# One set of the fifth group's first dense product by seven block products, in a fused linear-attention and GELU kernel

## The chip, the cores and the metric

The kernel runs on one core of one Trainium2 chip. The metric is device time in microseconds (us) of that core, from a few runs; a profile of one execution stands beside it. A core has four compute engines that run side by side: TensorE (PE in the profile, with its weight loads shown as PEld), VectorE (DVE), ScalarE (ACT) and GpSimd (POOL). SyncE (SP) issues the transfers. Matmuls write into PSUM, which has eight banks; all else lives in SBUF.

## The reference

The input of the dense part is the output of a chunked linear attention with a decay per head. Cut to what matters:

```python
# attention: B=4, H=8, S=768, D=64, blocks of 64
for b in range(nb):
    intra = einsum('bhic,bhjc->bhij', qb, kb) * Dmask        # causal, with decay
    out[b] = einsum('bhij,bhjd->bhid', intra, vb) + einsum('bhid,bhde->bhie', qb * lam_pow, kv_state)
    kv_state = lam_block * kv_state + einsum('bhsd,bhse->bhde', kb * rev_pow, vb)
# dense: 3072 tokens, d_model 512, d_ff 2048
x = out.transpose(0, 2, 1, 3).reshape(3072, 512)
h = x @ w_in                  # the first dense product
g = gelu_tanh(h)
y = g @ w_out                 # the second dense product
```

## The kernel before

The program interleaves the attention of 24 steps (each 256 positions of 4 heads) with the dense part of 7 groups of tokens. The dense work stands in a queue of small pieces, `filler`; `fill(n)` emits n of them between the attention's stages. Groups 3 to 6 have 512 tokens. Group 4 is the fifth, with steps 12 to 15.

A plain piece of the first dense product makes one block of 128 features for all 512 tokens: four matmuls of 512 columns and a gelu on ScalarE.

```python
SEVEN = (5, 6)                       # groups whose first dense product goes by seven products
groups = [[0, 1], [2], [3], [4, 5], [6, 7], [8, 9], [10, 11]]

def mm1(fs):
    Hps = ps_M.tile([P, per, N], FP32, tag="M", name="Hps")
    for i, f in enumerate(fs):
        for c in range(NC):                                   # NC = 4
            pin(nc.tensor.matmul(by_block(Hps[:, i, :]), w_in16[:, c, f * P : (f + 1) * P],
                                 x(c), start=(c == 0), stop=(c == NC - 1)))
    ...
    pin(nc.scalar.activation(out=dst, in_=Hps[:], func=AF.Gelu_apprx_tanh))
```

For groups 5 and 6 the first product is taken as a 2x2 block product with seven multiplications in place of eight (Strassen-Winograd). It needs sums of weight blocks (`sum_win`, made once on VectorE in fp16), four sums of activation blocks per group (`sum_x`), and evictions that add the seven products up. A *set* `k` is two feature blocks of each half. Three PSUM banks hold X, W and Y; three temporaries in SBUF hold what has been read out.

```python
X_FACTORS = {1: ((0, 0), (0, 0)), 2: ((0, 1), (1, 0)), 3: (4, (1, 1)), 4: ((1, 1), 4),
             5: (1, 1), 6: (2, 2), 7: (3, 3)}      # weight block, activation block; 1..4 alone are sums

def sum_x(m):                                      # xs, 4 of 128x512 fp16
    ...
    pin(nc.vector.tensor_tensor(x_block(m, cs), x_block(a, cs), x_block(b, cs), op))

def seven(m, k):
    ...                                            # four matmuls of 256 columns into
    dst = st[{2: "W", 5: "Y", 3: "Y"}.get(m, "X")] # X: 1, 6, 7, 4;  W: 2;  Y: 5, 3
    ...
    def copied(name, tag, eng):                    # a temporary out of the load buffers
        t = ld.tile([P, HH, 2, D], FP32, tag=tag, name=f"{name}_{g}_{k}")
        ...                                        # copy of dst into it, by eng
    if m == 1:   copied("m1", "q32", nc.scalar)
    elif m == 2: added(0, 0, "m1")                 # VectorE: m1 = W + m1; its gelu is kept for later
    elif m == 5: copied("q", "q32", nc.scalar); release()      # release: emits the gelus kept
    elif m == 6: copied("u2", "k32", nc.vector)
    elif m == 3: added(0, 1, "u2")
    elif m == 7: added(1, 1, "q")
    elif m == 4: pending.insert(0, lambda: gelu(1, 0, dst[:]))
    if k == HF // 2 - 1 and m in (3, 7, 4):
        release()
```

The load buffers are four each of `q32`, `k32` and `v32`, 128x512 fp32. They belong to the attention: a step's q, k and v are loaded into them, then cast to fp16 by three engines, transposed by a transfer, and used.

```python
ld = ctx.enter_context(tc.tile_pool(name="ld", bufs=4))
def cast_qk(s):
    ...
    pin(q_eng.tensor_tensor(wide(tq), q32[:], decay(dq, s), ALU.mult))           # VectorE
    pin(nc.scalar.activation(out=wide(tk), in_=k32[:], func=AF.Copy))            # ScalarE
def scale_v(s):
    pin(nc.gpsimd.tensor_tensor(wide(tv[:]), ld32[s][2][:], decay(dv, s), ALU.mult))  # GpSimd
def prep_v(s):       # scales v, then loads step s + 3
def prep_qk(s):      # cast_qk(s), then the transpose by a transfer
```

The second dense product goes by seven products in all these groups. It reads sums of gelu blocks, `gs`, that `sum_g` makes on VectorE: four sums over rows 0 to 3 and the same over rows 4 to 7. `behind(k, ...)` hangs such a sum on the k-th piece of the queue. For group 3 the last addition, `o` from `u` and `q`, is GpSimd's.

`burst(ns, ss)` emits the attention matmuls of two steps at once: scores S of steps `ns`, outputs O of steps `ss`, states K, and more of O; then the masking of S (`PT`, VectorE), the activations `xT` out of O (ScalarE), and the updates of the state: `t` on VectorE, `u` on GpSimd. Instructions keep the order in which they are written on each engine (`pin`). The schedule around group 4:

```python
    R(17, 15)                # its end queues group 4
    fill(1); U(17); fill(1)
    sum_win(3, 0, nc.vector);  fill(2)
    prep(19)
    sum_win(3, 1, nc.vector);  fill(2)
    sum_win(4, 0, nc.vector);  fill(2)
    sum_win(4, 1, nc.vector);  fill(2)
    prep_qk(20);  fill(1)
    prep_qk(21);  prep_v(20);  fill(3)
    burst((18, 19), (16, 17))
    prep_v(21);  fill(2)
    U(18);  U(19);  fill(4)
    prep_qk(22);  fill(2)
    burst((20, 21), (18, 19), 11, 4)         # queues group 5
    fill(3);  U(20);  U(21);  fill(20)
    prep_qk(23);  ...
```

Of the kernel before, what the change touches and what calls it, by code (L numbers as in the profile page):

```python
# [9 lines left out]
FP16 = mybir.dt.float16  # L10
AF = mybir.ActivationFunctionType
# [4 lines left out]
def kernel(  # L16
# [12 lines left out]
    P = 128  # L29
# [114 lines left out]
    def sum_win(m, j, eng):  # L144

        if not wi_sum:
            wi_sum.extend(wst.tile([P, 2, 2, DFF // 2], FP16, tag=f"w{2 + i}", name=f"ws{i}")
                          for i in range(2))
        a, op, b = I_SUMS[m]
        cs, fs = slice(0, 2), slice(512 * j, 512 * j + 512)  # L150
        pin(eng.tensor_tensor(w_in_block(m, cs, fs), w_in_block(a, cs, fs),
                              w_in_block(b, cs, fs), op))
# [96 lines left out]
    def wide(t):  # L249
        return t.rearrange("p j h d -> p h j d")  # L250

    def decay(t, s):
        hs = halves[s % 2]
        return t[:, hs, :].unsqueeze(3).to_broadcast([P, HH, 2, D])

    def prep_v(s):
        scale_v(s)
        if s >= 6:
            if s + 3 == FIRST_DMA_T + 1:
                load_step(s + 3, "qk")  # L260
            else:
                load_ahead(s + 3)
# [6 lines left out]
    def prep_qk(s):  # L269
        cast_qk(s)  # L270
        transpose_dma(s)

    def cast_qk(s):
        q32, k32, _ = ld32[s]
        tqk = a16p.tile([P, 2, 2, HH, D], FP16, tag="qk16", name=f"qk16_{s}")
        tq, tk = tqk[:, 0], tqk[:, 1]
        q_eng = nc.gpsimd if s == 3 else nc.vector
        pin(q_eng.tensor_tensor(wide(tq), q32[:], decay(dq, s), ALU.mult))  # L278
        if s == 0:
            inverse(halves[0])  # L280
            odd(halves[1])
            inverse(halves[1])
        pin(nc.scalar.activation(out=wide(tk), in_=k32[:], func=AF.Copy))  # L283
        a16[s] = (tq, tk)
        whole_qk[s] = tqk

    whole_qk = {}

    def transpose_dma(s):
        tqk = whole_qk.pop(s)  # L290
        if s >= FIRST_DMA_T:
            o = qkp.tile([P, 2, 2, 2, P], FP16, tag="qkT", name=f"qkT_{s}")
            pin(nc.sync.dma_start_transpose(out=o[:].rearrange("p a j h t -> p (a j h) t"),
                                            in_=tqk[:].rearrange("p a j h d -> p (a j h d)")))
            qkT[s] = o
            if s == FIRST_DMA_T:
                load_step(s + 1, "v")
# [219 lines left out]
        return gs_kept[1:]  # L517

    SEVEN = (5, 6)
    SLOTS = {5: {1: 0, 2: 1, 5: 1, 6: 1, 3: 1, 7: 1}, 4: {1: 0, 2: 1, 5: 0, 6: 1, 3: 1, 7: 1}}  # L520
    groups = [[0, 1], [2], [3], [4, 5], [6, 7], [8, 9], [10, 11]]
    group_of = {sb: (g, i) for g, sbs in enumerate(groups) for i, sb in enumerate(sbs)}
# [2 lines left out]
    def queue_group(g, lead=0, per_set=0):  # L525
# [69 lines left out]
        def product(m, p, part=None):  # L595

            st = of_group

            def bank(name):
                if name not in st:  # L600
                    st[name] = ps_M.tile([P, 1 if name == "X" else NP, HE], FP32, tag="M",
                                         name="M" + name[0])
                return st[name]

            if m in (2, 5, 3):
                dst = bank("Y" if m in (5, 3) else "W")[:, p]
            else:
                dst = bank(f"X{p}")[:, 0]
            opens = m == 1 or (m in (2, 5) and p == 0)
            closes = m in (2, 3, 4)  # L610
            a, b = FACTORS[m]
            for i in range(HF) if part is None else range(HF // 2 * part, HF // 2 * part + HF // 2):
                lhsT = g_rows(a, i)[:, p * P : p * P + P]
                if b in W_SUMS:
                    rhs = w_sum16[:, w_slot[b], i, :]
                else:
                    F, E = b
                    rhs = w_out16[:, F * HF + i, E * HE : E * HE + HE]
                pin(nc.tensor.matmul(dst, lhsT, rhs, start=(opens and i == 0),  # L619
                                     stop=(closes and i == HF - 1), skip_group_check=True))  # L620
            if part == 0:
                return
            last = p == NP - 1

            def temp(name):
                if name not in st:
                    st[name] = mtp.tile([P, NP, HE], FP32, tag=name, name=name)
                return st[name]

            def out_tile(T):  # L630
                if f"o{T}" not in st:
                    st[f"o{T}"] = otp.tile([P, NP, 2, HE], FP32, tag="o32", name=f"o{T}")
                return st[f"o{T}"]

            def copy(to, of):
                pin(nc.scalar.activation(out=to, in_=of, func=AF.Copy))  # L636

            def store(T, ps=slice(0, NP), es=slice(0, 2)):
                r = row0 + T * HN
                rows = out[r : r + HN, :].rearrange("(p q) (e d) -> q p e d", q=P, e=2)  # L640
                whole = g == 3
                for i in [ps] if whole else [slice(i, i + 1) for i in range(ps.start, ps.stop)]:
                    pin(nc.sync.dma_start(out=rows[:, i, es], in_=out_tile(T)[:, i, es, :]))

            one = slice(p, p + 1)
            if m == 1:
                copy(temp("m1")[:, p], dst)
            elif m == 2 and last:
                pin(nc.vector.tensor_tensor(out_tile(0)[:, :, 0, :], st["W"][:], st["m1"][:], ALU.add))
            elif m == 5 and last:  # L650
                copy(temp("q")[:], st["Y"][:])
            elif m == 6:
                copy(temp("u2")[:, p], dst)
            elif m == 3 and last:
                pin(nc.vector.tensor_tensor(out_tile(0)[:, :, 1, :], st["Y"][:], st["u2"][:], ALU.add))
                store(0)
            elif m == 7 and last_group:
                pin(nc.vector.tensor_tensor(out_tile(1)[:, p, 1, :], dst, st["q"][:, p], ALU.add))
                if last:
                    store(1, one, slice(1, 2))  # L660
            elif m == 7:
                copy(temp("u3")[:, p], dst)
                if last:
                    pin(nc.gpsimd.tensor_tensor(out_tile(1)[:, :, 1, :], st["u3"][:], st["q"][:],  # L664
                                                ALU.add))
# [32 lines left out]
        def seven(m, k):  # L698
# [48 lines left out]
                added(1, 1, "q")  # L747
            elif m == 4:
                pending.insert(0, lambda: gelu(1, 0, dst[:]))
            if k == HF // 2 - 1 and m in (3, 7, 4):  # L750
                release()

        def merge(lead, per_set):
# [83 lines left out]
        if g in SEVEN:  # L837
# [6 lines left out]
            for k, m in enumerate((2, 4, 3)):  # L844
                behind(len(parts) * k, 4, 8, (m,))
            return
        for i in range(HF):
            for fs in ([[i, i + HF]] if per == 2 else [[i], [i + HF]]):
                filler.append(lambda fs=fs: mm1(fs))
        for m, p in order:  # L850
# [4 lines left out]
        if per == 2:  # L855
            behind(5, 0, 4, (1, 2))
            behind(6, 0, 4, (4, 3))
            behind(7, 4, 8, (1,))
            behind(8, 4, 8, (2,))
            behind(9, 4, 8, (4,))  # L860
            behind(10, 4, 8, (3,))
        else:
            behind(9, 0, 4, (1, 2) if g == 3 else (1, 2, 4, 3))
            if g == 3:
                behind(12, 0, 4, (4, 3))
            w = 2 if g + 1 in SEVEN else 1
# [23 lines left out]
    def U(n):  # L890
        update(n, 1)
# [143 lines left out]
    U(17)  # L1035
    fill(1)
    sum_win(3, 0, nc.vector)
    fill(2)
    prep(19)
    sum_win(3, 1, nc.vector)  # L1040
    fill(2)
    sum_win(4, 0, nc.vector)
    fill(2)
    sum_win(4, 1, nc.vector)
    fill(2)
    prep_qk(20)
# [57 lines left out]
```

## Time and profile before

| what | value |
|---|---|
| time, median of 3 runs | 199.69 us (199.68 to 200.06) |
| span of the profiled execution | 198.0 us, TensorE clock 1.000 |
| TensorE, matmuls | 191.6 us busy, 97% of the span |
| VectorE, ScalarE, GpSimd | 153.9, 123.0, 75.5 us busy (78, 62, 38%) |
| plain first product, one matmul of 512 columns (as recorded) | 379 ns |
| seven-product matmul of 256 columns (as recorded) | 273 ns |
| sum of activations `xs`, VectorE | 0.41 us at the least |
| cast of q, VectorE / copy of 128x512 from PSUM, ScalarE | 0.68 / 0.60 us at the least |

Matmul records overlap, so their durations are not their cost; the distance from start to start is, and it is read from the chain or the timeline. The line of digits gives the busy tenths of an engine in 40 equal slices of the span. In the timeline a line is: start and duration in us, engine, source line, operation, result and operand, shapes and count; a bracket at its end gives the idle time of the engine just before, and what ended it. In the waits a line is: who waited for whom, the sum in us, how often, and the longest. The chain, followed back from the last instruction, gives start, duration and what ran.

### The profile page before, as it was taken

What the parts mean: (1) busy time and instruction counts of PE and PEld (TensorE: products, weight loads), DVE (VectorE), ACT (ScalarE), POOL (GpSimd) and SP (SyncE); (2) the same over time, 40 slices, a digit from 0 to 9 for tenths busy, and PEclk for the clock granted to TensorE, in tenths of its full rate; (3) what the DMA queues carried; (4) which work ended last, traced back from release to release, by engine and by line L of the source; (5) the groups of instructions that cost most, each with busy time, mean ns of one, the idle gap of its engine ahead of it and who ended that gap; (6) DMA issues with size and microseconds to landing.
All of it is one profiled execution on the core that took longest, in us unless ns stands there. A gap on an engine that the chain in (4) does not pass through costs nothing.

```text
span 198.0 us, 5937 instructions
## 1 busy us (share of the span) xinstructions
PE 191.6 (97%) x2439; PEld 140.2 (71%) x2439; DVE 153.9 (78%) x296; ACT 123.0 (62%) x251; POOL 75.5 (38%) x85
## 2 busy tenths in 40 slices
PE   8979999999999999999999999999999999999993
PEld 2546544456888888754588854578888888888882
DVE  4887722789999989969999927998778996588620
ACT  3673878457794675677645377844768836779221
POOL 6594213457557642465563526156002030002000
DMA  6999999999999999989994997400211200030205
GB/s 168 291 323 386 386 387 387 293 289 301 336 263 265 218 307 226 194 252 190 295 205 95 272 316 182 104 16 0 53 66 43 104 10 0 0 107 2 106 14 201
DMA packets 61722, 37.86 MB, mean 191 GB/s; under 512 B 17536, under 2 KB 54656, under 8 KB 61696
## 3 DMA queue, kind: packets, MB, share of 16 engines
q1 hardware_dynamic: 61152, 37.23, 72.9%
q8 instruction: 19, 0.31, 0.7%
q10 hardware_dynamic: 544, 0.26, 0.5%
q14 instruction: 7, 0.06, 0.1%
HBM read 27.26 MB, written 6.29 MB: 169 GB/s over the span
## 4 chain that ended last, share of the span: by engine, by line
PE 88%; SPq 4%; DMA 4%; ACT 1%; issue 1%
PE Hps L542 24%; PE MX L619 17%; PE MY L619 9%; PE HX L711 7%; PE O2ps L557 7%; PE MW L619 4%; DMA wi<-in_moe_w_in_dram 4%; SPq L70 4%; PE HY L711 4%; PE S L340 3%; PE Hps L802 3%; PE HW L711 2%; PE OK L398 2%; PE O L449 1%; PE O L424 1%; PE Tps L311 1%
## 5 line engine op out<-in xcount | busy, mean ns | idle before, releaser
L542 PE MATMUL Hps<-xT,w_in 128*128 128x512 f16 (+1 forms) x288 | 50.8, 332 | 0.0
L501 POOL TENSOR_TENSOR u<-t,lumask 128x256 f16<-128x256 f32 x40 | 31.0, 789 | 46.5 <-DVE t L494 28.4
L542 PEld LDWEIGHTS <-w_in 128*128 128x128 f16 x288 | 27.8, 98 | 19.0
L546 ACT ACTIVATE gT<-Hps 128x512 f16<-128x512 f32 x56 | 33.1, 598 | 9.3 <-PE Hps L542 8.8
L350 DVE TENSOR_TENSOR PT<-S,mask 128x512 f16<-128x512 f32 x48 | 30.3, 681 | 6.5 <-PE S L340 6.4
L619 PEld LDWEIGHTS <-gs 128*128 128x128 f16 x320 | 31.2, 98 | 3.6
L266 POOL TENSOR_TENSOR v<-v,dv 128x512 f16<-128x512 f32 x24 | 30.0, 1254 | 7.4 <-DMA v<-in_v_dram 7.2
L619 PEld LDWEIGHTS <-gT 128*128 128x128 f16 x240 | 23.2, 98 | 3.6 <-ACT gT L546 0.5
L619 PE MATMUL MX<-w_sum,gs 128*128 128x256 f16 x160 | 21.4, 273 | 0.0
L664 POOL TENSOR_TENSOR o<-u,q 128x512 f32<-128x512 f32 (+1 forms) x5 | 5.8, 1158 | 37.9 <-ACT u L636 37.9
L278 DVE TENSOR_TENSOR qk<-q,dq 128x512 f16<-128x512 f32 x23 | 19.7, 859 | 0.6 <-DMA q<-in_q_dram 0.5
L283 ACT ACTIVATE qk<-k 128x512 f16<-128x512 f32 x24 | 15.0, 626 | 6.5 <-DMA k<-in_k_dram 6.4
L589 DVE TENSOR_TENSOR gs<-gT 128x1024 f16<-128x1024 f16 (+1 forms) x24 | 17.6, 737 | 1.5 <-ACT gT L546 1.5
L557 PE MATMUL O2ps<-w_out,gT 128*128 128x512 f16 x64 | 14.6, 379 | 0.0
L475 ACT ACTIVATE xT<-OK 128x256 f16<-128x256 f32 x26 | 10.0, 453 | 7.3 <-PE OK L398 7.1
L711 PEld LDWEIGHTS <-ws 128*128 128x128 f16 x128 | 12.5, 98 | 1.8
L636 ACT ACTIVATE u<-MX 128x256 f32<-128x256 f32 x18 | 6.9, 384 | 10.2 <-PE MX L619 10.2
L475 ACT ACTIVATE xT<-O 128x256 f16<-128x256 f32 x22 | 8.0, 459 | 5.9 <-PE O L449 5.0
L557 PEld LDWEIGHTS <-gT 128*128 128x128 f16 x64 | 6.1, 98 | 6.6
L619 PE MATMUL MY<-w_out,gs 128*128 128x256 f16 x80 | 10.7, 273 | 0.0
L340 PEld LDWEIGHTS <-qkT 64*64 64x64 f16 x384 | 6.0, 106 | 6.5 <-issue 2.5
L589 DVE TENSOR_TENSOR gs<-gs,gT 128x1024 f16<-128x1024 f16 (+1 forms) x12 | 10.2, 851 | 0.3
(95 smaller groups left out, 319.4 us busy)
## 6 DMA issues: line engine op xcount, KB each, us to landing
q<-in_q_dram SPq DMA_DIRECT2D x24, 256.0 KB, 5.0
k<-in_k_dram SPq DMA_DIRECT2D x24, 256.0 KB, 5.2
v<-in_v_dram SPq DMA_DIRECT2D x23, 256.0 KB, 5.4
out_dram<-o SPq DMA_DIRECT2D x19, 256.0 KB, 4.3
wo<-in_moe_w_out_dram SPq DMA_DIRECT2D x4, 1024.0 KB, 9.5
wi<-in_moe_w_in_dram SPq DMA_DIRECT2D x4, 512.0 KB, 7.0
wi<-in_moe_w_in_dram SPq DMA_DIRECT2D x2, 1024.0 KB, 12.8
out_dram<-o SPq DMA_DIRECT2D x2, 512.0 KB, 6.6
```

Of the source, the lines that this page charges most:

```text
L266: pin(nc.gpsimd.tensor_tensor(wide(tv[:]), ld32[s][2][:], decay(dv, s), ALU.mult))
L278: pin(q_eng.tensor_tensor(wide(tq), q32[:], decay(dq, s), ALU.mult))
L283: pin(nc.scalar.activation(out=wide(tk), in_=k32[:], func=AF.Copy))
L350: pin(nc.vector.tensor_tensor(t[:, hl].rearrange("p b c d -> p b (c d)"), Sps[:].rearrange("p b c d -> p b (c d)"), mask[:].unsqueeze(1).t ...
L475: pin(nc.scalar.activation(out=d, in_=o, func=AF.Copy))
L501: pin(nc.gpsimd.tensor_tensor(u[:], state[half][:].unsqueeze(2).to_broadcast([P, 2, 2, D]), lumask[:, 2 * half : 2 * half + 2, :].unsqueez ...
L542: pin(nc.tensor.matmul(by_block(Hps[:, i, :]), w_in16[:, c, f * P : (f + 1) * P], x(c), start=(c == 0), stop=(c == NC - 1)))
L546: pin(nc.scalar.activation(out=dst, in_=Hps[:], func=AF.Gelu_apprx_tanh))
L557: pin(nc.tensor.matmul(O2[tau][0][:], gT[:, f % HF, f // HF, tau * P : (tau + 1) * P], w_out16[:, f, :], start=(n == 0), stop=(n == NF - 1)))
L589: pin(nc.vector.tensor_tensor(g_rows(m, i), g_rows(a, i), g_rows(b, i), op))
L619: pin(nc.tensor.matmul(dst, lhsT, rhs, start=(opens and i == 0), stop=(closes and i == HF - 1), skip_group_check=True))
L711: pin(nc.tensor.matmul(dst[:, i, :], w_in_block(a, slice(c, c + 1), slice(f * P, f * P + P))[:, 0], x_block(b, slice(c, c + 1))[:, 0], sta ...
```

## The change

Set 0 of group 4's first dense product (feature blocks 0, 1, 8 and 9) goes by seven block products, to spare TensorE one multiplication in eight of that set; the other twelve blocks stay plain. The seven pieces are interleaved with plain ones (a 0 in the list is a plain piece), and their gelus are released at once. The rest makes room: the key casts of steps 20 and 21 move forward, the activation sums and the query casts are placed by hand, the transposes of steps 20 and 21 part from their casts, the cast of step 22 moves behind the second burst, the gelu sums of group 4 are hung on other pieces (two of them behind the second burst), and the first output tile of group 3 is stored in two transfers.

```diff
+    def cast_q(s):
+        both16(s)                     # the fp16 tile of q and k, made once
+        q_eng = nc.gpsimd if s == 3 else nc.vector
+        pin(q_eng.tensor_tensor(wide(a16[s][0]), ld32[s][0][:], decay(dq, s), ALU.mult))
+    def cast_k(s):
+        both16(s)
+        pin(nc.scalar.activation(out=wide(a16[s][1]), in_=ld32[s][1][:], func=AF.Copy))
...
+    MIXED = 4
...
-                whole = g == 3
+                whole = g == 3 and T == 1
...
-            if k == HF // 2 - 1 and m in (3, 7, 4):
+            if (k == HF // 2 - 1 or g == MIXED) and m in (3, 7, 4):
                 release()
...
-        for i in range(HF):
+        if g == MIXED:
+            sum_xs.append(sum_x)
+            plain = [[f] for i in range(2, HF) for f in (i, i + HF)]
+            for m in (1, 2, 5, 0, 6, 3, 0, 7, 0, 4):
+                filler.append((lambda m=m: seven(m, 0)) if m else (lambda fs=plain.pop(0): mm1(fs)))
+            for fs in plain:
+                filler.append(lambda fs=fs: mm1(fs))
+        for i in range(HF) if g != MIXED else ():
...
-            behind(9, 0, 4, (1, 2) if g == 3 else (1, 2, 4, 3))
+            n1 += 3 * (g == MIXED)
+            behind(n1 - 7, 0, 4, (1, 2))
             if g == 3:
                 behind(12, 0, 4, (4, 3))
+            else:
+                behind(n1 + 5, 0, 4, (4,))
+                behind(n1 + 9, 0, 4, (3,))
...
     sum_win(3, 0, nc.vector)
+    cast_k(20)
     fill(2)
     prep(19)
     sum_win(3, 1, nc.vector)
     fill(2)
     sum_win(4, 0, nc.vector)
     fill(2)
+    cast_k(21)
     sum_win(4, 1, nc.vector)
-    fill(2)
-    prep_qk(20)
-    fill(1)
-    prep_qk(21)
+    for m in (1, 2, 3, 4):
+        sum_xs[0](m)
+    cast_q(20)
+    transpose_dma(20)
     prep_v(20)
     fill(3)
+    cast_q(21)
+    fill(7)
     burst((18, 19), (16, 17))
+    transpose_dma(21)
     prep_v(21)
-    fill(2)
+    fill(3)
     U(18)
     U(19)
-    fill(4)
-    prep_qk(22)
-    fill(2)
+    fill(3)
     burst((20, 21), (18, 19), 11, 4)
     fill(3)
     U(20)
     U(21)
+    prep_qk(22)
     fill(20)
```

More of the change, by code (lines that the diff above doesn't have):

```diff
@@ L273, in cast_qk @@
     def cast_qk(s):
[L274 to L278, printed above, removed]
+        cast_q(s)
         if s == 0:
@@ L282, in cast_qk, with both16 @@
             inverse(halves[1])
-        pin(nc.scalar.activation(out=wide(tk), in_=k32[:], func=AF.Copy))
-        a16[s] = (tq, tk)
-        whole_qk[s] = tqk
+        cast_k(s)
+    def both16(s):
+        if s in a16:
+            return
+        tqk = a16p.tile([P, 2, 2, HH, D], FP16, tag="qk16", name=f"qk16_{s}")
+        a16[s] = (tqk[:, 0], tqk[:, 1])
+        whole_qk[s] = tqk
+    def cast_q(s):
[5 more added lines that the diff above has]
+        pin(nc.scalar.activation(out=wide(a16[s][1]), in_=ld32[s][1][:], func=AF.Copy))
     whole_qk = {}
@@ L519 @@
     SEVEN = (5, 6)
+    MIXED = 4
+    sum_xs = []
     SLOTS = {5: {1: 0, 2: 1, 5: 1, 6: 1, 3: 1, 7: 1}, 4: {1: 0, 2: 1, 5: 0, 6: 1, 3: 1, 7: 1}}
```

## The prediction, made before the changed kernel had run

> **What bounds the kernel now.** I read the page's head first, then TensorE's waits, then the chain, then VectorE and GpSimd instruction by instruction around the change (110 to 137 us).
>
> ```profile
> PE 191.6 (97%) x2439; PEld 140.2 (71%) x2439; DVE 153.9 (78%) x296; ACT 123.0 (62%) x251; POOL 75.5 (38%) x85
> ...
> PE   8979999999999999999999999999999999999993
> ...
> DVE  4887722789999989969999927998778996588620
> ```
>
> TensorE is busy for 97% of the span and in every slice after the third. A busy matmul record can hide a wait, so the waits of TensorE come next:
>
> ```profile
> PE S L340 <- DVE qkT L316: 0.8, 2, 0.5
> PE idle L181 <- PEq L1088: 0.8, 1, 0.8
> PE OK L398 <- POOL u L501: 0.6, 1, 0.6
> PE Tps L311 <- POOL qk L278: 0.4, 1, 0.4
> PE Hps L802 <- ACT w_in L108: 0.4, 1, 0.4
> ```
>
> That is 3.0 us in all, none of it in the changed stretch. The chain there is TensorE alone, without a gap:
>
> ```profile
> 109.45 3.49 PE MX L619 x32
> 112.95 4.32 PE Hps L542 x20
> 117.26 0.57 PE S L340 x32
> ```
>
> So a matmul removed here is time gained, and any wait put in is time lost: nothing later has slack to give it back. The second thing to see is VectorE just before the fifth group (group 4 in the code) starts, with GpSimd beside it:
>
> ```profile
> 108.45 1.53 DVE L151 TENSOR_TENSOR ws<-w_in 128x1024 f16<-128x1024 f16 x1
> 109.90 0.68 DVE L655 TENSOR_TENSOR o<-MY,u 128x512 f32<-128x512 f32 x1
> 110.50 1.27 DVE L151 TENSOR_TENSOR ws<-w_in,ws 128x1024 f16<-128x1024 f16 x2
> 111.70 2.35 DVE L278 TENSOR_TENSOR qk<-q,dq 128x512 f16<-128x512 f32 x2
> 117.66 2.48 DVE L350 TENSOR_TENSOR PT<-S,mask 128x512 f16<-128x512 f32 x4 [3.60 <-PE S L340]
> ```
> ```profile
> 107.94 1.49 POOL L266 TENSOR_TENSOR v<-v,dv 128x512 f16<-128x512 f32 x1
> 111.70 1.81 POOL L664 TENSOR_TENSOR o<-u,q 128x512 f32<-128x512 f32 x1 [2.27 <-ACT u L636]
> 113.47 1.49 POOL L266 TENSOR_TENSOR v<-v,dv 128x512 f16<-128x512 f32 x1
> ```
>
> A bracket would mark idle time. VectorE has none from 94.9 until 114.06; then it rests 3.6 us. It is a backlog that ends just too late to serve group 4's first matmul, at 112.78 in the timeline.
>
> **What the Trainium skill says.** "SBUF — State Buffer", section "SBUF: two separate sides": VectorE and GpSimd share a port pair under an exclusive lock; a VectorE instruction with two SBUF inputs and a GpSimd one wait for each other to end. The trace agrees: ws, usually 0.68, takes 1.53 while v is scaled (107.94 to 109.43); of the two casts at 111.70 the first takes 0.68 and the second 1.75, as o sits between them. They take turns. The sum from PSUM at 134.28 takes its usual 0.68 beside such a scaling. "TensorE: Matmul & The Clock Gate", section "Wait — 56ns, not 53.3ns?": start to start is the columns over 2.4 GHz plus about 2.5 ns, which makes 216 and 109 ns for 512 and 256 columns. The trace: 16 of 512 in 3.45 us, 4 of 256 in 0.44. The same page, section "What's actually happening", puts TensorE at half rate after an idle window of about 3.4 us. The trace shows no more than a wait of 1.5 us near 74, after which eight products still take 0.87.
>
> **The change, part by part.** *Removed and added on TensorE.* One set covers four feature blocks. Plain, that is 16 matmuls of 512 columns, 3.45 us. By seven products it is 28 of 256, 7 x 0.44 = 3.06. Gain 0.40 us, all on the path.
>
> *Added on VectorE:* four sums of activations (0.41 each, 0.34 to the next) and four evictions of 0.69, some 4.1 us; on ScalarE two copies of 0.60, while the gelus keep their number. Neither is a bound by its sum; where they stand matters. As built, VectorE's order after 111.70 is: four sums, q cast 20, sum on HW, q cast 21, copy of HX, sums on HY and HX.
>
> *The new chain.* The seven products need three temporaries, and they take load buffers. The one for product 1 is the buffer that held q of step 20, and the one for product 5 that of step 21; so the ScalarE copies of products 1 and 5 wait for the q casts 20 and 21. Product 6 writes over the bank of product 1, and product 3 adds into that of product 5, so each waits for that copy. The key casts moved early free the key buffer; the query casts can't be early, because VectorE is late.
>
> Undisturbed, TensorE from 112.78 runs 1, 2, 5, a plain block, 6, 3: product 3 would start 4 x 0.437 + 0.864 = 2.61 later, at 115.40. VectorE with the locks: first sum ends 112.05; o runs (1.15) to 113.2; second sum to 113.5; v of step 20 runs (1.0) to 114.5; third and fourth to 115.2; cast 20 to 115.8. ScalarE copies product 1 until 116.5. The sum on HW ends 117.2, cast 21 at 117.8, the copy of product 5 at 118.4. Product 3 starts at about 118.45: 3.05 us late in two waits (product 6 first). Without any lock: sums 1.4, cast 0.6, copy 0.6, sum 0.6, cast 0.6, copy 0.6 and hops of 0.15 from 111.70 make 116.3, 0.9 late. I see no way to less.
>
> *Behind it:* the burst's K matmul takes the bank of the third plain block, whose gelu now stands behind the gelus of products that came late: another 0.25.
>
> *Second place.* The sums of gelus for group 4's second product move behind the burst of steps 20 and 21, and so does q cast 22. Counted from that burst's first S (125.92 in the kernel before): VectorE reaches these at 6.48. Before, the copy of HX in group 5's first set ends at 12.1 (137.32 + 0.68), and product 7 that needs it starts at 12.5. After, three more instructions of 0.6 stand ahead of it, 1.8 us, while TensorE brings one more plain block (0.86), a margin of 0.43 and 0.32 of VectorE idle time. That alone is a wait of 0.2. But in this stretch GpSimd makes two u and scales v twice (132.17 to 136.7), and with their turns taken: cast 22 until 7.45, gs 8.6, gs 10.25, gs 11.9, then six of 0.6 until 15.5. Product 7 would start at 13.4, so up to 2.2 lost.
>
> *Hidden:* the order of key casts (ScalarE is 62% busy), o of group 3 stored in two pieces, and the transpose of step 21, which goes out behind the first burst as before and lands 3.1 later, some 2 us ahead of its S.
>
> Sum with all locks: -0.40 + 3.05 + 0.25 + 2.2 = +5.1. With none: -0.40 + 0.9 + 0.25 + 0.2 = +0.95. The locks are in the trace, so I stand nearer the first, but turns can fall more kindly than I set them: **+4.2, 203.9 us**.
>
> **The rivals.** First, that VectorE keeps up, TensorE stays the bound, and the change brings its 0.4: 199.3. For it: VectorE is 78% busy overall and rests 3.6 us before the burst. Against it: that rest begins at 114.06, after the work was needed. Second, that only the first place waits: the gelu sums need not be late if GpSimd's turns fall elsewhere; then some +2.9, 202.6. For it: the 0.32 idle and 0.43 margin; against: three more instructions in a stretch without idle time. Third, a transfer as the new wait (transpose 20 or 21, or load 23 behind a store): against it, at 3.1 us to landing there are about 2 us to spare; it would add 0 to 1. Fourth, a wait long enough to halve TensorE's clock, which would add up to 1.7 (an estimate from the clock-gate page's window of 3.4 us at half rate); my two waits before product 3 are split by work.
>
> **The range and the chances.** The floor of my argument is +0.9, the full sum +5.1. 8 times in 10: 201.6 to 205.4, that is no less than most of the first place and no more than the full sum and a bit. Two per cent slower begins at 203.68, just under my time; so slower has 0.53 and same 0.46. Faster by two per cent would need ten times the matmul time removed: 0.01.
>
> **What would show it.** Of TensorE's waits after, products 6 and 3 of group 4 should wait for ScalarE's copies (0.4 to 1.5, and 1 to 2 us), which wait for VectorE's casts; VectorE's sums and casts from 111.7 on should last over 0.41 and 0.68 beside o and v. In group 5's first set, product 7 should wait for VectorE's copy. Group 4's 28 products should start 109 ns apart where nothing waits. If product 3 starts before 115.5, my chain is wrong; if it is late and the total is not, something behind had slack that the chain view did not show me.

## The result, and the profile after

The changed kernel takes **207.7 us** (median of 6 runs, 206.43 to 210.27) against 199.88 us of the kernel before on the same chip: a ratio of 1.035, 95% interval 1.031 to 1.040. The ratio leaves out two slow executions, 209.93 and 210.27 us (the profile of the first lost 2.6 us before group 4 began); the other four take 206.43 to 207.79, median 207.0, so the change costs about 7.2 us. The prediction was 203.9 us with a range up to 205.4: the direction was right, the size too small.

The profile shown here is of a repeat of the changed kernel (207.55 us, ratio 1.036, 1.032 to 1.040; the profiled execution took 207.68), which stood beside the first experiments. Its page has, in the same order as the one before: busy times and the busy tenths in 40 slices of 5.1 us. PEclk is the clock that TensorE was granted, in tenths.

```profile
PE 194.0 (94%) x2449; PEld 142.1 (69%) x2451; DVE 161.6 (78%) x304; ACT 123.8 (60%) x253; POOL 74.8 (36%) x85
...
PE   8979999999999999999999499997999999999992
...
DVE  5897525689999899789999839999678997588620
...
PEclk9999999999999999999999969999999999999999
```

The row of nines of TensorE is broken twice, at slice 23 (a 4, from 113 us) and slice 28 (a 7, from 139 us). The slice after the first hole is full again, but there the clock row has a 6: TensorE is busy and slow. TensorE's waits from 110 us on (waiter, releaser, sum, times, longest); before, this stretch had none:

```profile
PE HX L723 <- DVE u L736: 1.4, 1, 1.4
PE HY L723 <- ACT q L734: 1.4, 1, 1.4
PE HX L723 <- ACT m L734: 1.2, 1, 1.2
PE MX L631 <- ACT u L648: 0.4, 1, 0.4
PE K L448 <- ACT o L648: 0.2, 1, 0.2
```

From below: product 6 waits for ScalarE's copy of product 1 (`m`), product 3 for that of product 5 (`q`), and product 7 of group 5's first set for VectorE's copy of HX (`u`). Products 6 and 3 are the first place of the prediction, product 7 the second. The last two lines are not in it. A wait is shorter here than what it costs from start to start, because a record of a matmul is longer than its step; all sums below are start to start.

The timeline of the first place, VectorE, GpSimd, ScalarE and TensorE mixed (start, duration, what; a bracket is idle time just before):

```profile
111.58 0.41 DVE L702 TENSOR_TENSOR xs<-xT 128x512 f16<-128x512 f16 x1
111.58 1.54 POOL L676 TENSOR_TENSOR o<-u,q 128x512 f32<-128x512 f32 x1 [2.27 <-ACT u L648]
...
112.02 1.38 DVE L702 TENSOR_TENSOR xs<-xT,xs 128x512 f16<-128x512 f16 x1
...
113.08 1.22 POOL L266 TENSOR_TENSOR v<-v,dv 128x512 f16<-128x512 f32 x1
...
113.33 1.26 DVE L702 TENSOR_TENSOR xs<-xT 128x512 f16<-128x512 f16 x1
...
114.84 0.68 DVE L291 TENSOR_TENSOR qk<-q,dq 128x512 f16<-128x512 f32 x1
...
115.60 0.60 ACT L734 ACTIVATE m<-HX 128x512 f32<-128x512 f32 x1 [2.35 <-DVE qk L291]
...
116.25 0.60 PE L723 MATMUL HX<-xs,ws 128*128 128x256 f16 x4 [1.25 <-ACT m L734]
...
116.84 0.68 DVE L291 TENSOR_TENSOR qk<-q,dq 128x512 f16<-128x512 f32 x1
...
117.61 0.60 ACT L734 ACTIVATE q<-HY 128x512 f32<-128x512 f32 x1 [1.41 <-DVE qk L291]
...
118.25 0.60 PE L723 MATMUL HY<-xT,ws 128*128 128x256 f16 x4 [1.41 <-ACT q L734]
...
118.69 1.75 PE L554 MATMUL Hps<-xT,w_in 128*128 128x512 f16 x4
```

A sum of activations takes 0.41 us alone and 1.38 or 1.26 beside GpSimd's `o` and `v`. ScalarE stands idle for 2.35 us until the cast of q of step 20 has read the buffer that its copy is to write, then 1.41 for step 21. And the last line: a plain piece, four matmuls recorded as 1.03 us before, is recorded as 1.75. That is the halved clock, seen by stretches (busy time of TensorE, granted clock, share of DMA, GB/s):

```profile
112.00:116.00 4.00, 3.00 (x24) 1.00 1.19 260
116.00:119.00 3.00, 1.34 (x10) 0.97 1.22 193
119.00:123.00 4.00, 4.00 (x40) 0.59 1.19 313
123.00:138.00 15.00, 14.90 (x265) 1.00 0.16 31
```

Cut finer, in stretches of 0.2 us, the granted clock is 0.50 from 118.9 to 122.1 us and 1.00 from 122.3 on: half speed for 3.4 us, which costs half of that.

The second place is VectorE's copy of HX for group 5's first set, and product 7, which needs it:

```profile
143.76 0.68 DVE L736 COPY u<-HX 128x512 f32<-128x512 f32 x1
144.49 0.60 PE L723 MATMUL HX<-xs,ws 128*128 128x256 f16 x4 [1.45 <-DVE u L736]
```

The chain of the work that ended last, before all TensorE here, now leaves it for what the prediction named (start, duration, what):

```profile
116.85 0.68 DVE qk L291
117.61 0.61 ACT q L734
118.25 0.60 PE HY L723 x4
118.85 1.59 PE Hps L554 x4
```

(One step earlier it names a store of `o` that landed at 116.85. VectorE was at the sum on HW from 116.23 and took the cast at its usual 0.61 after it, so I don't read the store as the cause.)

The account from the start of group 4 (112.78 before, 112.67 after) to the start of the last group of 32 matmuls (191.04 and 198.21): 78.26 us before, 85.54 after, 7.28 more.

| where | us more | predicted |
|---|---|---|
| 28 products for 16 plain matmuls | -0.40 | -0.40 |
| first place: product 6 late by 1.41, product 3 by 1.56 | 2.97 | 3.05 |
| behind it, two plain pieces and product 7 at the halved clock | 1.70 | 0 (a rival, put at up to 1.7 and dismissed) |
| first burst (K matmul) | 0.30 | 0.25 |
| second place: product 7 of group 5's first set | 1.61 | 2.2 |
| product 4 of that set, behind VectorE's cast of step 23 | 0.28 | not seen |
| third place: attention output of steps 22/23 by 0.45, MX pieces of group 5 near 187 us by 0.49 | 0.94 | not seen |
| sum | 7.40 | 5.1, of which 4.2 chosen |

The remaining 0.6 us of the 7.9 us between the spans (198.0 and 205.9) lie outside this stretch: group 4 starts 0.1 us earlier, and from the start of the last group to the end it takes 7.7 us for 6.9. The thirteen profiles of this study, before included, take 6.8 to 8.0 us there; I see no edit that this part follows.

### The profile page after: what moved, and what is told of

Same layout as the page of the kernel before. It is cut to its first block, busy times and chain, and to the rows that moved or that the text cites. A ratio compares the mean times of both kernels' runs of the same rounds, so it can differ in the third digit from the quotient of the medians.

```text
span 208.1 us, 5973 instructions
## 1 busy us (share of the span) xinstructions
PE 194.6 (93%) x2451; PEld 141.9 (68%) x2451; DVE 161.5 (78%) x304; ACT 123.9 (60%) x253; POOL 73.9 (35%) x85
## 4 chain that ended last, share of the span: by engine, by line
PE 58%; DVE 16%; DMA 9%; ACT 6%; SPq 5%; issue 4%; DVEq 0%; ACTq 0%
PE Hps L554 16%; PE MX L631 9%; PE O2ps L569 7%; PE MY L631 6%; PE HX L723 5%; SPq L70 4%; DMA wi<-in_moe_w_in_dram 4%; DVE PT L360 3%; DVE gs L601 3%; PE Hps L814 3%; PE MW L631 3%; DMA qkT<-qk 2%; DMA q<-in_q_dram 2%; PE S L350 2%; ACT gT L740 2%
## 5 line engine op out<-in xcount | busy, mean ns | idle before, releaser
L554 PE MATMUL Hps<-xT,w_in 128*128 128x512 f16 (+1 forms) x272 | 49.0, 335 | 0.0
L554 PEld LDWEIGHTS <-w_in 128*128 128x128 f16 x272 | 26.6, 99 | 17.4 <-issue 1.0
L558 ACT ACTIVATE gT<-Hps 128x512 f16<-128x512 f32 x52 | 30.8, 599 | 8.3 <-PE Hps L554 7.9
L266 POOL TENSOR_TENSOR v<-v,dv 128x512 f16<-128x512 f32 x24 | 29.1, 1214 | 8.6 <-DMA v<-in_v_dram 5.9
L631 PEld LDWEIGHTS <-gT 128*128 128x128 f16 x240 | 23.2, 98 | 4.1 <-issue 0.6
L601 DVE TENSOR_TENSOR gs<-gT 128x1024 f16<-128x1024 f16 (+1 forms) x24 | 20.8, 868 | 1.5 <-ACT gT L558 1.5
L291 DVE TENSOR_TENSOR qk<-q,dq 128x512 f16<-128x512 f32 x23 | 19.0, 826 | 1.7 <-DMA q<-in_q_dram 1.6
L723 PEld LDWEIGHTS <-ws 128*128 128x128 f16 x144 | 14.2, 99 | 7.2 <-issue 5.2
L723 PE MATMUL HX<-xs,ws 128*128 128x256 f16 x72 | 11.3, 281 | 2.6 <-DVE u L736 1.5
L723 PEld LDWEIGHTS <-w_in 128*128 128x128 f16 x108 | 10.5, 98 | 1.5 <-issue 0.3
L350 PE MATMUL S<-qkT 64*64 64x128 f16 x384 | 9.2, 221 | 2.1 <-DMA qkT<-qk 1.3
```

The costliest lines, as they stand in the source:

```text
L291: pin(q_eng.tensor_tensor(wide(a16[s][0]), ld32[s][0][:], decay(dq, s), ALU.mult))
L350: pin(nc.tensor.matmul(Sps[hl][half64(c), hp, jk, :], o[half64(hl), 1, jk, hp, half64(c)], o[half64(hl), 0, :, hp, half64(c)], start=True, ...
L601: pin(nc.vector.tensor_tensor(g_rows(m, i), g_rows(a, i), g_rows(b, i), op))
L723: pin(nc.tensor.matmul(dst[:, i, :], w_in_block(a, slice(c, c + 1), slice(f * P, f * P + P))[:, 0], x_block(b, slice(c, c + 1))[:, 0], sta ...
```

## The experiments

All ratios are to the kernel before, run beside them on the same chip. "Clock" is TensorE's mean granted clock over a whole execution; it is 0.987 to 0.992 where it was halved behind a wait, and else 0.995 or more.

### The changed kernel once more

No edit.

> The changed kernel once more, beside the other three on one chip, for a profile without a late start. Two-waits theory: about 206.5 us where the clock stays at 1.0; products 6 and 3 of group 4's set wait for ScalarE's copies 2.5 to 3 us together, and product 7 of group 5's first set waits for VectorE's copy 1.5 to 2.5 us. The rival, that the loss comes from late transfers: TensorE waits over 1 us for a transpose near the first burst here too.

Measured: 207.55 us, 1.036 (1.032 to 1.040). Three of the four executions have a clock of 0.988 to 0.992 and take 207.4 to 207.8; one has 1.000 and takes 206.21. So the halved clock comes in some executions only, and is worth 1.2 to 1.6 us of time. The waits don't depend on it: the profile with one piece more, below, has both at full clock. The rival of late transfers is out, since from 110 us on TensorE waits for no transfer in this profile.

### The moves alone

```diff
-            for m in (1, 2, 5, 0, 6, 3, 0, 7, 0, 4): ...    # set 0 plain, like the others
-            n1 += 3 * (g == MIXED)
-    for m in (1, 2, 3, 4):
-        sum_xs[0](m)
-    fill(7)
+    fill(4)
```

> All the moves stay, but set 0 is plain again: no sums of activations, no temporaries for group 4. It leaves nothing of the reference out. Two-waits theory: the first place goes (no copies into load buffers), the second stays, since the gelu sums and the cast of step 22 still stand behind the second burst: about 200.4 to 202, with the wait of product 7 in group 5's first set of 0.2 to 2. Rival (the moves cost nothing, the set costs all): 199.7 within 0.3.

Measured: 202.49 us, 1.014 (1.010 to 1.017). Without one block product, the moves of casts and sums cost 2.5 us by themselves, somewhat more than the 200.4 to 202 that I had expected. Its waits from 110 us on:

```profile
PE S L350 <- DMA qkT<-qk: 0.7, 1, 0.7
PE HX L723 <- DVE u L736: 0.7, 1, 0.7
PE MX L631 <- ACT u L648: 0.4, 1, 0.4
PE K L448 <- ACT o L648: 0.2, 1, 0.2
```

Nothing of the first place is there: it needs the products. The second is (0.88 and 0.28 us, start to start), and so is the whole third place, 0.94: those come from the moves. New is that the second burst waits 0.9 us for the transpose of step 21. The prediction gave that transfer 3.1 us to landing and 2 us to spare. Here it went out at 119.53 and took 6.4 us, where the kernel before has 3.1. The change had put the loads of step 23 and a store of `o` (issued from 115.05 to 118.62) right ahead of it; before, these loads stood behind. In the changed kernel it went out at 124.63, some 5 us after them, landed in 3.3 us, and nothing waited.

### The temporaries in buffers that no pending cast reads

```diff
-                copied("q", "q32", nc.scalar)
+                copied("q", "v32" if g == MIXED else "q32", nc.scalar)
-    prep_v(20)                 # scales v of 20 and loads step 23
+    scale_v(20)
     fill(3);  cast_q(21);  fill(7)
+    load_ahead(23)             # so the temporaries take step 19's buffers
```

> The changed kernel with the loads of step 23 behind the seven products, so that their temporaries lie in the buffers of step 19, whose casts are long done; all else stays. Two-waits theory: products 6 and 3 wait no more for casts 20 and 21; product 7 of that set still waits about 1 us for VectorE's copy of HX, which stands behind the casts. Some 2 to 3 us faster than the changed kernel. Rival (VectorE is late by its work alone, whatever the buffers): less than 0.5 us faster.

Measured: 203.59 us, 1.018 (1.016 to 1.020), 4.0 us less than the changed kernel on the same chip. VectorE's order and its slow sums are as they were; TensorE's first place is now this:

```profile
114.85 0.60 PE L723 MATMUL HX<-xs,ws 128*128 128x256 f16 x4
115.28 0.60 PE L723 MATMUL HY<-xT,ws 128*128 128x256 f16 x4
115.72 1.03 PE L554 MATMUL Hps<-xT,w_in 128*128 128x512 f16 x4
117.39 0.60 PE L723 MATMUL HX<-xs,ws 128*128 128x256 f16 x4 [0.64 <-DVE u L736]
```

Products 6 and 3 start on time, at 114.85 and 115.28. What is left is 0.81 us at product 7, whose copy is VectorE's and stands behind the casts. The clock is 0.998 to 1.000 in all four executions. So the buffers alone take away 2.2 of the 2.97 us of the first place and the 1.7 us of the clock. The first burst pays 0.4 us back, as its K matmul now waits for a gelu; in the traces that makes 3.45 us to the start of the last group, for 4.0 between the medians.

### GpSimd's sum and scaling behind the first burst

```diff
+    held_o = []                          # o of group 3 and its store
-    prep_v(20)
+    load_ahead(23)
     fill(3);  cast_q(21);  fill(7);  burst((18, 19), (16, 17))
+    for f in held_o: f()                 # first run: ahead of transpose 21
     transpose_dma(21)
+    for f in held_o: f()                 # second run: behind it instead
+    scale_v(20)
     prep_v(21)
```

> The changed kernel with GpSimd's addition of group 3's output and its scaling of v of step 20 behind the first burst, so that the four sums of activations and the two casts on VectorE have the shared port to themselves. Port-lock theory: the four sums take 1.4 to 1.5 us in place of 3.5, product 3 starts some 2 us earlier, and the kernel is 1.5 to 2.5 us faster than the changed one. Rival (the order of VectorE and the buffers alone make the wait): less than 0.5 us.

Measured: 206.64 us, 1.032 (1.029 to 1.035). This one is confounded. The first place shrank to one wait of 1.0 us, but the store of `o` now stood ahead of the transpose of step 21 in the queue, and the second burst waited for it:

```profile
126.26 0.42 PE L350 MATMUL S<-qkT 64*64 64x128 f16 x16
129.32 0.64 PE L350 MATMUL S<-qkT 64*64 64x128 f16 x16 [2.64 <-DMA qkT<-qk]
129.75 1.07 PE L434 MATMUL O<-PT,v 64*64 64x128 f16 x32
```

Behind that wait the clock is halved as well (0.50 from 129.4 to 132.6 us), and 0.989 to 0.992 over the whole of three of four executions. The next run mends the order.

> GpSimd's sum o of group 3 and its scaling of v of step 20 run behind the first burst, as in gpsimd_late, but the transpose of step 21 is issued ahead of the store of o, so that it doesn't queue behind it. My theory: about 2 of the 3.0 us of the first place are turns that VectorE loses to GpSimd; the first place falls to about 1.0 us, and with no wait of over 1.1 us there TensorE's clock is not halved behind it: 2 us less than the changed kernel where its clock stayed whole, up to 3.8 less where it was halved, 203.8 to 205.6. Rival: the casts are late by their order alone, and the turns only shift them: less than 0.8 us gained.

Measured: 204.77 us, 1.025 (1.021 to 1.028), clock 0.995 to 1.000. VectorE, with GpSimd out of the way:

```profile
112.33 0.41 DVE L711 TENSOR_TENSOR xs<-xT 128x512 f16<-128x512 f16 x1
112.77 0.42 DVE L711 TENSOR_TENSOR xs<-xT,xs 128x512 f16<-128x512 f16 x1
113.11 0.42 DVE L711 TENSOR_TENSOR xs<-xT 128x512 f16<-128x512 f16 x1
113.45 0.42 DVE L711 TENSOR_TENSOR xs<-xT,xs 128x512 f16<-128x512 f16 x1
113.78 0.69 DVE L291 TENSOR_TENSOR qk<-q,dq 128x512 f16<-128x512 f32 x1
```

Four sums in 1.45 us start to start, for 3.26 in the changed kernel. Product 6 is on time and product 3 is 1.03 us late; the prediction's sum without any lock said 0.9. So without turns lost to GpSimd the first place is 1.9 us shorter, and 1.0 stays with the order of the casts. This 1.9 and the 2.2 of the buffers overlap and don't add: the turns make the casts late, the buffers tie the copies to the casts, and undoing either breaks the same chain. The work put off is not free: a K matmul of the second burst waits for the late scaling of v, 0.65 us.

### The gelu sums and the cast of step 22 where they were

```diff
-            behind(n1 - 7, 0, 4, (1, 2))
+            behind(n1 - 7, 0, 4, (1, 2) if g == 3 else (1, 2, 4, 3))
-            else:
-                behind(n1 + 5, 0, 4, (4,))
-                behind(n1 + 9, 0, 4, (3,))
-    fill(3);  burst((20, 21), (18, 19), 11, 4)
+    fill(2);  prep_qk(22);  fill(1);  burst((20, 21), (18, 19), 11, 4)
```

> The changed kernel with its second place undone: the four gelu sums of group 4's products all hang on the pieces they had before, and the cast of q and k of step 22 is ahead of the second burst again. My theory: product 7 of group 5's first set waited 1.6 us, and the next plain step 0.3, only because VectorE was given these three pieces of work behind the second burst; then this wait goes and the time falls by 1.5 to 1.9 us against the changed kernel. Rival: the wait came from the lateness carried over from the first place, and stays when the work is moved back: less than 0.4 us. The first place (products 6 and 3 of group 4, 3.0 us) stays in both.

Measured: 206.53 us, 1.031 (1.027 to 1.036), some 0.7 to 1.0 us under the changed kernel (medians of two chips, with the halved clock in two of four executions here and in three of four there; 0.44 us in the traces, from the start of group 4 to the start of the last group). That is less than the 1.5 to 1.9 that I had expected. The waits:

```profile
PE HY L723 <- ACT q L734: 1.4, 1, 1.4
PE Hps L554 <- DVE PT L360: 1.3, 1, 1.3
PE HX L723 <- ACT m L734: 1.2, 1, 1.2
```

The wait for `u` of group 5 is gone while the first place stays, so the moved work was its cause and not the lateness carried over. But a plain piece now waits 1.3 us for the mask sums of the second burst (`PT`), which stand behind the gelu sums put back. Of 1.9 us, 1.4 came back there: in either place this work of VectorE is waited for.

### One plain piece more behind the second burst

```diff
     burst((20, 21), (18, 19), 11, 4)
-    fill(3);  U(20);  U(21)
+    fill(4);  U(20);  U(21)
```

> The changed kernel with one more piece between U(19) and the second burst (4 for 3), so that the later queue of pieces stands against the later steps as it did before the change. My theory: the attention output of the pair 22/23 (0.88 for 0.45 us) and the eight matmuls of the third group-5 stage near 187 us (1.44 for 0.95) wait only because everything behind the burst moved by one piece against VectorE's and ScalarE's work; the time falls by 0.5 to 0.9 us. Rival: these waits belong to the two moved gelu sums or are a matter of chance from run to run; then the change is below 0.3 us.

(The expectation names the place wrongly: the piece was added behind the second burst, ahead of U(20).) Measured: 205.15 us, 1.028 (1.024 to 1.032). Both waits of the third place are gone from the trace, 0.94 us: the attention output of steps 22/23 takes 0.45 us to the next group again. So are the 0.28 us at product 4 of group 5's first set, 1.2 us in all: VectorE's cast of step 23 stands behind the sum on HX again, and not ahead of it. The medians differ by more, because only one of four executions has the halved clock; the three with a clock of 0.996 or more take 204.7 to 205.2, the three such of the changed kernel in its two runs 206.2 to 206.5, so 1.0 to 1.3 us, as the kernel before was 0.3 us faster on this chip. The third place is the shift of the later queue against the steps: the set of seven left one plain piece more to be run before group 5, and all behind stood one piece later against VectorE and ScalarE. The rival, the two moved gelu sums, is out: the run before this one moves them back and keeps both waits.

### A plain piece between the two waits

```diff
-            for m in (1, 2, 5, 0, 6, 3, 0, 7, 0, 4):
+            for m in (1, 2, 5, 0, 6, 0, 3, 7, 0, 4):
```

> The changed kernel with the second plain piece moved between product 6 and product 3 (1, 2, 5, 0, 6, 0, 3, 7, 0, 4 for 1, 2, 5, 0, 6, 3, 0, 7, 0, 4); VectorE's order and ScalarE's copies stay. My theory: products 6 and 3 wait as long for their copies as before, until about 116.3 and 118.3, so the second wait falls from 1.56 to some 0.7 us and 0.86 us are gained; and with 1.3 us of work between the two waits TensorE's clock is not halved behind them, which gives another 1.2 to 1.8 us in the executions in which it was: the mean clock is 0.995 or more, 205.4 to 205.8 us. Rival: the halved clock of the changed kernel has nothing to do with its waits and falls on some executions of any order: then the clock is still near 0.99 in about half of the executions, and those take 206.5 to 207.

Measured: 205.47 us, 1.029 (1.027 to 1.030). TensorE's first place:

```profile
116.24 0.60 PE L723 MATMUL HX<-xs,ws 128*128 128x256 f16 x4 [1.25 <-ACT m L734]
116.67 1.03 PE L554 MATMUL Hps<-xT,w_in 128*128 128x512 f16 x4
118.24 0.60 PE L723 MATMUL HY<-xT,ws 128*128 128x256 f16 x4 [0.54 <-ACT q L734]
118.67 0.60 PE L723 MATMUL HX<-xs,ws 128*128 128x256 f16 x4
119.11 1.03 PE L554 MATMUL Hps<-xT,w_in 128*128 128x512 f16 x4
```

Products 6 and 3 start within 0.01 us of where they started in the changed kernel (116.25 and 118.25), so the chain of casts and copies is untouched; 0.86 us of plain work has moved into the second wait. And the plain piece at 119.11 is recorded as 1.03, at full speed. The same stretch of 5 us in both, the changed kernel first, then this one:

```profile
118.00:123.00 5.00, 4.75 (x44) 0.66 0.99 260
```
```profile
118.00:123.00 5.00, 4.49 (x122) 1.00 1.05 291
```

All four executions have a clock of 0.996 to 1.000. In the traces the stretch from group 4 to the last group is 2.4 us shorter than in the changed kernel: 0.86 and 1.70, less 0.2 at the first burst.

How often the clock was halved (0.992 or less):

| kernels | executions |
|---|---|
| the two waits with one product between them (the changed kernel and its repeat, gelu sums back, one piece more) | 10 of 18 |
| no such pair (own buffers, moves alone, GpSimd's second run, this one, the three versions below) | 1 of 44 |
| the kernel before, run beside them | 1 of 48 |

GpSimd's first run, with its single wait of 2.64 us, is not in the table.

So it comes with the pair of waits, in about half of the executions; why only in half is not shown. That work between the waits spares the clock rests on these four executions, which at 10 in 18 would all escape by chance about once in 26 times. The edit also shortened the two waits together from 2.97 to 2.1 us, so it doesn't tell their length from their distance.

### Can the set be had without the waits?

Three versions put together what the runs above showed. The first, called reworked in the expectations:

```diff
+                copied("q", "v32" if g == MIXED else "q32", nc.scalar)   # own buffers
+            behind(n1 - 7, 0, 4, (1, 2) if g == 3 else (1, 2, 4, 3))     # sums as before
+    scale_v(20);  fill(3);  fill(4);  cast_q(20);  transpose_dma(20)
+    fill(3);  cast_q(21);  load_ahead(23)
     burst((18, 19), (16, 17));  transpose_dma(21);  ...
+    fill(2);  prep_qk(22);  fill(2);  burst((20, 21), (18, 19), 11, 4)
```

> The seven products with none of what made TensorE wait: temporaries in buffers that no pending cast reads, the casts of q of steps 20 and 21 behind the evictions of the products, the gelu sums and the cast of step 22 where they were before the change, and the number of plain pieces ahead of each burst as before. My theory: what stays is the gain of 28 matmuls of 256 columns for 16 of 512, 0.40 us: 199.3 to 199.9, 0.998 of the kernel before. Rival: one of the places has a further cause that these moves don't touch (VectorE's four sums and four evictions, 4.1 us more work ahead of the first burst): 200.4 to 202.

Measured: 200.55 us, 1.0039 (1.0024 to 1.0054): 7 us better than the changed kernel, and still 0.8 behind the kernel before, in the range of the rival. None of the three places waits, and the seven products take 0.44 us each. But two new ones stand in the bursts (the second line is the weight load of S):

```profile
PE K L448 <- ACT gT L558: 0.3, 1, 0.3
...
PEld L350 <- DMA qkT<-qk: 0.3, 1, 0.3
```

K of the first burst waits for the gelu of the third plain piece, which ScalarE reaches behind the gelus of the products (0.5 us start to start); S of the second waits for the transpose of step 21, which now stood behind the load of step 23 and took 5.8 us to land (0.34), and the step behind it takes 0.24 more. The expectation of the next run took the first of these for the mask sums; the waits name the gelu.

The second adds one plain piece ahead of the first burst (`fill(4)` for the `fill(3)` ahead of `cast_q(21)`, one less behind) and puts `load_ahead(23)` behind `transpose_dma(21)`:

> reworked with two of its remaining waits taken away: a fourth plain piece ahead of the first burst (two for three behind it), so that the mask sums of the first burst are not behind the casts of q of steps 20 and 21, and the load of step 23 behind the transpose of step 21 instead of ahead of it. My theory: reworked lost 0.5 us to the mask sums in the first burst and 0.34 us to the transpose in the second, out of the 1.16 us by which it missed its own gain; without them 199.5 to 199.9 us, as the kernel before or a little under it. Rival: the four sums and four evictions more (4.1 us of VectorE) have to be paid for in this stretch in one place or another, and a wait appears elsewhere: 200.3 or more.

Measured: 202.24 us, 1.013 (1.012 to 1.015). Both waits shrank or went (K to 0.21, S to none, with the transpose landing in 3.7 us). Others came: product 4 starts 0.36 us late, waiting for VectorE's sum on HX, and at the second burst a plain piece waits 0.8 us for VectorE's mask sums. The rival holds. In the trace, from group 4 to the last group, this kernel loses 0.4 us to the first; the rest of the 1.7 us by which its median is above it lies behind the last matmuls and between executions (201.57 to 202.60), and I can't assign it.

The third leaves the first's pieces as they are, makes product 6's copy on ScalarE, and puts the load behind the transpose:

> reworked with one eviction less on VectorE: product 6's copy of HX is made by ScalarE, so that VectorE reaches the casts of q and the mask sums of the first burst 0.69 us sooner; and the load of step 23 stands behind the transpose of step 21. My theory: the 0.5 us of the first burst and the 0.34 us of the second go, ScalarE having 0.7 us of idle time at that place: 199.5 to 199.9 us. Rival, after reworked2: VectorE's (and now ScalarE's) added work has to be paid for in one place or another: 200.2 or more.

Measured: 201.51 us, 1.0085 (1.005 to 1.012). ScalarE makes that copy at 116.70, behind a gelu, where VectorE of the first version made it at 115.35; product 7 waits for it 0.5 us, and both bursts wait again, the first for a gelu and the second for mask sums. The rival holds here too. No version beat the kernel before.

## Why the prediction was wrong, point by point

**The steps that failed.** Two terms of the sum were set to nothing. The fourth rival was dismissed because "my two waits before product 3 are split by work": the halved clock came behind these waits and cost 1.70 us where it came. And "Hidden" held no shift of the later queue, which cost 1.22 us (0.28 and 0.94). The terms that the prediction did name came to 4.48 us, for its sum of 5.1. Even at full clock the changed kernel takes 206.2 to 206.5 us, above the range; the shift, and 0.6 us at the two ends of the span, were enough for that.

**What bounds the kernel: right.** TensorE had no slack behind the change, and each wait put in was paid in full: the terms of the account add up to 7.40 us for 7.28 measured.

**The 0.40 us of the products: right.** In the changed kernel each group of four starts 0.44 us after the one before, where nothing waits.

**The first place: right in mechanism and size.** Predicted: sums end at 115.2, cast 20 at 115.8, copy at 116.5, cast 21 at 117.8, copy at 118.4, product 3 at 118.45. In the timeline: 114.9, 115.5, 116.2, 117.5, 118.2, 118.25; VectorE began 0.12 earlier than set. Own buffers took the two waits away, and GpSimd put off took two thirds of them away. The 0.25 at the first burst measured 0.30. At full clock (the profile with one piece more) K waits there for the gelu, as predicted; in the profile at halved clock the chain names the first mask sum instead. "I see no way to less" than 0.9 was wrong: it is so for that order and those buffers, and own buffers with the casts behind the evictions had no wait there.

**The second place: right, a little too large.** VectorE reached cast 22 at 6.47 us after the second burst's first S (predicted 6.48), the copy of HX ended at 14.9 (predicted 15.5), as the gelu sums beside GpSimd took 1.10, 1.42 and 1.52 and not a full turn each time. Product 7 was 1.61 us late for "up to 2.2".

**The choice of 4.2 from a sum of 5.1: nearly right, for the terms that it holds.** These came to 4.48 us (-0.40, 2.97, 0.30, 1.61). In the first place the turns fell as worked out; in the second they fell more kindly, by 0.6. This is 0.3 of the 3.7 us by which the profiled execution missed (7.9 between the spans for 4.2); nearly all the rest is what the sum left out.

**The fourth rival, dismissed for the wrong reason: 1.7 us of the trace.** I wrote of the halved clock that "my two waits before product 3 are split by work". The split is one product of 0.44 us between waits of 1.41 and 1.56, and behind them the clock was halved for 3.4 us; with 1.3 us of work between them it was not, in four executions. The size was right: "up to 1.7" for 1.70 measured. I had read the Trainium skill's "TensorE: Matmul & The Clock Gate", section "What's actually happening", as a rule about one unbroken idle window of about 3.4 us. The waits here, with the product, are 3.4 us long with 0.44 of work in them, and the measurement decides: an unbroken idle window isn't needed. The same page warns of this in its section "A second HAM failure mode: psum-queue depth-cycling" (short idle times between groups of matmuls throttle the clock as well), which I did not use. That the window runs freely, as the page also says, would fit that half of the executions escape; no run here shows it.

**The third place, not foreseen: 0.94 us.** Under "Hidden" I listed transfers and key casts, and did not carry on the list of pieces: TensorE runs three plain pieces before the first burst, five between the bursts and four behind the second, where it had run five, eight and three. There is one more to run behind the second burst, and everything after it meets the later steps one piece later. The moves alone show it, and one piece more there takes it away, together with the 0.28 us at product 4, which belong here too.

**The transfer as a rival:** "some 2 us ahead of its S" was wrong by 3 us for the moves alone, where the transpose of step 21 took 6.4 us to land and S waited 0.9. I had taken 3.1 us from the kernel before, where the load of step 23 stood behind this transpose, and the change puts it ahead. The three versions bear this out: 5.8 us with the load ahead, 3.7 and 3.3 with it behind. In the changed kernel the late first place let the loads pass long before.

What remains of the miss, some 0.6 us, lies at the two ends of the span, and stays open.

## What to carry to other kernels

Where TensorE is the bound without slack, count for a change what it adds to the other engines in its own stretch against their idle time there: here some 4 us of VectorE work for 0.40 us of TensorE, in a stretch where VectorE had rested 4.7 us (3.60 and 1.05 in the timeline before, from 111 to 131 us), and each order that I tried paid some of it as a wait. A temporary that takes a rotating buffer inherits the readers of its last owner: look up which instruction that is before placing the copy. Having found the waits, add up how densely they stand: two waits with little between them can cost once more through the clock, and a piece of work put between them gained 1.5 to 2.1 us here (by the ratios and by the medians), 0.86 of it because the second wait was filled.

## What the hardware showed that I had not expected

TensorE's clock was halved behind 3.0 us of waits in two parts with 0.44 us of work between (0.59 granted from 119 to 123 us; from a plain piece to the next piece it took 1.54 us instead of 0.86), in 10 of 18 executions. So it was behind one wait of 2.64 us, in three of four. In each of the four profiles that show it, it lasted 3.4 us. Behind single waits of 1.0 to 1.6 us (GpSimd's second run, and product 7 of group 5's first set) no profile shows it.
